# First token tiles of a layernorm, GLU and long-convolution kernel: loads in halves of 64 partitions, VectorE copies, wide warm-up matmuls, another issue order

## The chip, the cores and the metric

The kernel runs on one core of a Trainium2 chip. TensorE (PE) multiplies matrices, VectorE (DVE) and ScalarE (ACT) work on elements and empty PSUM, SyncE (SP) issues nearly all DMA transfers; ScalarE issues a few at the start. The metric is the device time of one execution in microseconds (us). Three executions of the kernel before took 243.47, 243.84 and 244.39 us; their median, 243.84 us, is the time before.

## The reference

A sequence of 2048 tokens of 640 channels goes through a layernorm. The normalised tokens `xn` feed two branches, and the result is the sum of the input and both:

```python
x  = A_q                                     # (1, 2048, 640) bf16
xn = _layernorm(x)
out = x + _A_ref(xn, A_k, A_v, ...) + _B_ref(xn, B_w_gate, B_w_up, B_w_down)

def _A_ref(q, k, v, shift_k, ssm_k, ssm_D):
    kv = causal_conv4(k, shift_k) * v        # per channel, 4 taps
    y  = irfft(rfft(kv) * rfft(ssm_k))       # causal convolution over 2048 positions
    return q * (y + kv * ssm_D)

def _B_ref(x, w_gate, w_up, w_down):         # 640 -> 1728 -> 640
    return (sigmoid(x @ w_gate) * (x @ w_up)) @ w_down
```

## The kernel before

**Tiling.** The 2048 tokens are 16 tiles of 128 (`acc[:, m, :]`, one row of 640 channels on each partition). Partition 32q+n of tile m holds token 64n+16q+m, which is why a tile's load is written as four pieces of 32 partitions, one for each q (`load_x`, line 365). Four tiles make a group `tr`; there are four groups.

**Branch B.** For a group, the four normalised tiles are transposed into `xnT` (640 channels on the partitions, 512 tokens). Group 0 is transposed on PE (`rec_tp`, five 128x128 transposes to a tile at line 704, then one copy from PSUM to `xnT0`, lines 328 and 329); groups 1 to 3 are written to DRAM and read back with a transposing DMA (line 698). Then 14 column blocks `fc` of gate and up are multiplied (`rec_fc`, line 773, five matmuls of 512 columns for each of gate and up), evacuated by a sigmoid on ACT (line 734) and a product on DVE (line 736) into `hT`, and multiplied by the down weights (`rec_down`, line 789). Blocks 0 and 1 of group 0 are done tile by tile instead (`rec_first`, line 752), so that PE can begin when the first token tile is there.

**Branch A.** The convolution is a two-step Fourier transform as matmuls, in ten slices: `rec_st1` (line 508), `rec_st2` (line 528), products on DVE, `rec_st3` (line 576), and `rec_st4` (line 608) at the end.

**Order.** Every piece of work is recorded as an operation with the buffers it reads and writes (`_Plan.op`). The list `ORDER` gives the order in which all operations are emitted; `ON_DVE` names those that may run on ACT or DVE and run on DVE. Each engine runs its own operations strictly in that order, and so does each queue of DMA issues. A PSUM tile of tag `g` (two slots) or `c` (three slots) has to be emptied before its slot is used again. DMA issues use eight semaphores in turn: an issue waits until the transfer issued eight before it has landed.

**The start, where the change is.** A memset makes a zero tile, and PE multiplies it 61 times with 84 columns (`warm`, line 818, operation `("wps", 0)`). Tiles 0 and 1 of the tokens are loaded in quarters, q = 0 and 1 from SP, q = 2 and 3 from ACT; tiles 2 and 3 come together, in quarters from SP. On SP the fourth piece of tiles 0 and 1 stands behind the first gate weights, and the pieces of tiles 2 and 3 behind that. Statistics of tiles 0 to 2 are taken by DVE (`rec_stat`: two `bn_stats` at line 638 and one `bn_aggr` at 640), those of tile 3 by ACT (`rec_stat_act`: a sum at line 645 and a sum of squares at 651). `rec_fast` is a square root on ACT (line 656) and a reciprocal on DVE (658); `rec_norm` (682) normalises on DVE. The copies of the transposes of tiles 0 and 2 are on ACT, those of 1 and 3 on DVE. A second set of 12 zero matmuls of 85 columns follows the first transpose.

Of the kernel before, what the change touches and what calls it, by code (L numbers as in the profile page):

```python
# [44 lines left out]
def _dft_tables():  # L45
# [31 lines left out]


ORDER = [
# [38 lines left out]
]  # L118
ON_DVE = [
    38, 47, 101, 105, 138, 139, 141, 145, 148, 150, 181, 183, 198, 221, 319, 412, 439, 446, 469, 483, 487, 505, 517, 808  # L120
]


# [94 lines left out]
def kernel(  # L218
# [116 lines left out]
    def dma(fn, nd, run, q="SP", few=0.0, **kw):  # L335
        few = few or (1.4 if nd <= 64 and run > 1000 else 1.0)
        plan.op({q: (0.48 + nd / 8000.0, lambda: fn(nc.sync if q == "SP" else nc.scalar))},
                size=1.05 * few * nd * (10.6 + run / 23.8) / 16e3 + 0.03, nd=nd, **kw)
# [26 lines left out]
    def load_x(q, m0, m1, eng, pri):  # L365
        dma(lambda e: e.dma_start(acc[32 * q:32 * q + 32, m0:m1, :], xq4[q][:, m0:m1, :]), 32, 1280 * (m1 - m0), q=eng,  # L366
            w=[("acc", m, q) for m in range(m0, m1)], pri=pri)

    def weight(tr, n):
        tr = 0 if tr == 1 else tr  # L370
# [272 lines left out]
    def rec_stat_act(m0, m1, pri):  # L643
        for m in range(m0, m1):
            plan.op({"ACT": (0.75, lambda m=m: nc.scalar.activation(jk, acc[:, m, :], ACT.Identity,  # L645
                                                                    accum_out=st[:, TMP, m:m + 1]))},
                    r=[("acc", m, q) for q in range(4)] + [("jk",)], w=[("sum", m)], pri=pri)
        act(100, lambda: nc.scalar.activation(st[:, MEAN, m0:m1], st[:, TMP, m0:m1], ACT.Copy, scale=1.0 / DM),
            r=[("sum", m) for m in range(m0, m1)], w=[("mean", m) for m in range(m0, m1)], pri=pri)
        for m in range(m0, m1):  # L650
            plan.op({"ACT": (0.75, lambda m=m: nc.scalar.activation(jk, acc[:, m, :], ACT.Square, scale=-1.0,
                                                                    bias=st[:, MEAN, m:m + 1], accum_out=st[:, VAR, m:m + 1]))},
                    r=[("acc", m, q) for q in range(4)] + [("mean", m), ("jk",)] + ([("sd", 1)] if m == 3 else []), w=[("mv", m)], pri=pri)

    def rec_fast(m, pri, scale=1.0):
        act(100, lambda: nc.scalar.activation(st[:, TMP, m:m + 1], st[:, VAR, m:m + 1], ACT.Sqrt, bias=eps, scale=scale),
# [80 lines left out]
                r=[pk(1), (sg,)], w=[(hk, fc)], pri=pri - 2000)  # L737

    MG, MD = 213.5, 135.0
    WARM = (61, 84)  # L740

    def rec_first(pri):
        every = [(fc, u) for fc in range(2) for u in range(2)]
# [62 lines left out]
    FIX = -1e6  # L806
# [9 lines left out]
    def warm(n, w=512):  # L816
        for _ in range(n):
            nc.tensor.matmul(tl["wps"][:, 0, 0:w], lhsT=tl["warm"][:, 0:P], rhs=tl["warm"][:, 0:w], start=True, stop=True)
    plan.op({"PE": (4.4, lambda: warm(*WARM))}, r=[("warm",)], w=[("wps", 0)], alloc=[("wps", "c")], pri=FIX)
    for m in range(2):  # L820
        for q in range(2):
            load_x(q, m, m + 1, "SP", FIX)
            load_x(q + 2, m, m + 1, "ACT", FIX)
    load_w(0, 0, FIX + 2)
    load_w(0, 1, FIX + 2)
    for q in range(4):
        load_x(q, 2, 4, "SP", FIX + 1)
    dma(lambda e: e.dma_start(FEt, Fdram.ap()[:, 2 * K1:]), 128, 256, w=[("FE",)], pri=11.0, nb=9.0)
    dma(lambda e: e.dma_start(Ft[:], Fdram.ap()[:, 0:2 * K1]), 128, 128, w=[("F",)], pri=12.0, nb=9.0)
    load_D(10.0)  # L830
# [17 lines left out]
    rec_fast(3, FIX + 50, 1.0 / DM)  # L848
    rec_norm(0, FIX + 5, True)
    rec_tp(0, FIX, True)  # L850
    plan.op({"PE": (1.5, lambda: warm(12, 85))}, r=[("warm",), ("xn0", 0)], w=[("wps", 1)], pri=FIX + 0.5)
    for m0, m1, k in ((4, 8, "LS1"), (8, NQ, "LNS")):
        if m0 == 4:
            for m in range(m0, m1):
# [77 lines left out]
```

## Time and profile before

| | us |
|---|---|
| median of three executions | 243.84 |
| the profiled execution: its own time | 244.01 |
| the profiled execution: span from first to last instruction | 242.2 |
| PE busy | 232.5 |
| DVE busy | 198.4 |
| ACT busy | 152.0 |
| first matmul of `rec_first` (line 752) starts | 7.87 |
| first matmul of `rec_fc` (line 773) starts | 14.13 |
| last matmul ends | 236.78 |

The profile is of one execution. Times in it run from its first instruction; 1.8 us of the execution's own time lie outside the span. The granted clock is the share of full speed that the throttle gave to TensorE. "DMA share" is the mean busy share of the core's 16 DMA engines in a stretch of time.

### The profile page before, as it was taken

The page shows a single profiled execution, that of the slowest core. Times are in us where ns is not written, and L with a number is a line of the kernel's source. Part 1 is how long each engine was busy: PE and PEld are TensorE (multiplying, and loading weights), DVE is VectorE, ACT ScalarE, POOL GpSimd, SP SyncE. Part 2 cuts the span into 40 slices and gives each one's busy share as a digit, 9 for nine tenths or more (in the row PEclk, how much of TensorE's full clock was granted, in tenths as well). Part 3 has the DMA queues.
Part 4 walks back from the last instruction along what each step waited for, and adds up shares of the span by engine and source line. Part 5 has one row for each costly group of instructions (what it writes and reads, how often), then busy time and mean ns, then how long its engine had stood idle before and what let it go on. Part 6 is the DMA issues. An engine that isn't in the chain of part 4 may idle for free.

```text
span 242.2 us, 8395 instructions
## 1 busy us (share of the span) xinstructions
PE 232.5 (96%) x3739; PEld 142.7 (59%) x3739; DVE 198.4 (82%) x281; ACT 152.0 (63%) x213; POOL 0.7 (0%) x6
## 2 busy tenths in 40 slices
PE   7799999999999999999999999999999999999990
PEld 7764445774445556766646455777665645456760
DVE  3616975697899998999999998898988799879971
ACT  2542333058777999167998989879797752663310
POOL 1000000000000000000000000000000000000000
PEclk9799999999999999999999999999999999999998
DMA  5999999999989699996998794399561888520771
GB/s 156 271 232 283 238 220 214 283 160 150 184 157 191 103 185 189 192 289 86 158 199 185 201 187 156 87 299 151 147 168 22 216 245 296 141 83 3 202 243 48
DMA packets 92667, 43.72 MB, mean 180 GB/s; under 512 B 69720, under 2 KB 89112, under 8 KB 92312
## 3 DMA queue, kind: packets, MB, share of 16 engines
q1 hardware_dynamic: 92440, 43.04, 80.8%
q8 instruction: 29, 0.48, 0.8%
q10 hardware_dynamic: 192, 0.16, 0.2%
q14 instruction: 6, 0.05, 0.1%
HBM read 30.74 MB, written 5.24 MB: 149 GB/s over the span
## 4 chain that ended last, share of the span: by engine, by line
PE 87%; DMA 5%; ACT 3%; DVE 1%; issue 1%; SPq 1%; ACTq 0%
PE g L773 47%; PE g L789 19%; PE c L528 9%; DMA acc<-in_A_q_dram 5%; PE c L576 4%; PE c L508 3%; PE c L752 3%; PE c L608 2%; ACT VV L645 2%; SPq L366 1%; PE g L704 0%; DVE bs L638 0%; DVE VV L682 0%; DVE hT L736 0%; ACT xnT L328 0%
## 5 line engine op out<-in xcount | busy, mean ns | idle before, releaser
L773 PE MATMUL g<-xnT,w 128*128 128x512 bf16 x380 | 88.6, 380 | 0.4 <-ACT sig L734 0.4
L789 PE MATMUL g<-wd,hT 128*128 128x320 bf16 (+2 forms) x462 | 65.0, 295 | 0.0
L773 PEld LDWEIGHTS <-w 128*128 128x128 bf16 x380 | 35.3, 98 | 40.0 <-issue 1.0
L789 PEld LDWEIGHTS <-hT 128*128 128x128 bf16 x462 | 43.0, 98 | 17.0 <-issue 0.2
L328 ACT CAST S<-c 128x1024 bf16<-128x1024 f32 (+2 forms) x41 | 39.8, 1001 | 9.5 <-PE c L528 5.3
L736 DVE TENSOR_TENSOR hT<-sig,g 128x512 bf16<-128x512 bf16 x44 | 30.1, 685 | 16.3 <-PE g L773 14.7
L734 ACT ACTIVATE sig<-g 128x512 bf16<-128x512 f32 x44 | 26.2, 601 | 25.2 <-PE g L773 23.0
L773 PE MATMUL g<-xnT,VV 128*128 128x512 bf16 x140 | 32.2, 379 | 0.0
L328 ACT CAST T<-c 128x1024 bf16<-128x1024 f32 (+1 forms) x21 | 20.6, 1009 | 9.7 <-PE c L508 6.3
L482 DVE TENSOR_TENSOR P<-kt,sT 128x2048 bf16<-128x2048 bf16 x20 | 24.3, 1221 | 0.2
L528 PEld LDWEIGHTS <-Mt 64*128 64x128 f16 x1280 | 19.8, 95 | 5.7 <-issue 5.4
L528 PE MATMUL c<-T,Mt 64*128 64x64 bf16 x1280 | 22.2, 190 | 0.5 <-issue 0.5
L773 PEld LDWEIGHTS <-VV 128*128 128x128 bf16 x140 | 13.3, 98 | 15.0
L800 DVE TENSOR_TENSOR acc<-g,acc 128x320 bf16<-128x320 f32 (+2 forms) x33 | 15.7, 479 | 7.3 <-PE g L789 7.0
L328 ACT CAST VV<-c 128x1024 bf16<-128x1024 f32 x17 | 17.0, 1019 | 4.9 <-PE c L576 4.7
L331 ACT ACTIVATE T<-c 128x1024 bf16<-128x1024 f32 x18 | 18.1, 1026 | 1.3 <-PE c L508 1.3
L645 ACT ACTIVATE VV<-acc 128x640 bf16<-128x640 bf16 x9 | 6.6, 737 | 12.2 <-DMA acc<-in_A_q_dram 12.1
L560 DVE TENSOR_TENSOR S<-S 64x2048 bf16<-64x2048 bf16 x10 | 12.2, 1220 | 0.3
L557 DVE TENSOR_TENSOR S<-S 128x2048 bf16<-128x2048 bf16 x10 | 12.2, 1224 | 0.3
L562 DVE TENSOR_TENSOR S<-P 64x2048 bf16<-64x2048 bf16 x10 | 12.2, 1222 | 0.3
L486 DVE TENSOR_TENSOR P<-P,P 128x2048 bf16<-128x2048 bf16 x10 | 12.2, 1223 | 0.2
L550 DVE TENSOR_TENSOR P<-S,P 128x2048 bf16<-128x2048 bf16 x10 | 12.2, 1220 | 0.0
(75 smaller groups left out, 183.0 us busy)
## 6 DMA issues: line engine op xcount, KB each, us to landing
P<-S SPq DMA_DIRECT2D x20, 256.0 KB, 3.8
w<-in_B_w_up_dram SPq DMA_DIRECT2D x7, 640.0 KB, 6.3
w<-in_B_w_gate_dram SPq DMA_DIRECT2D x7, 640.0 KB, 6.3
kt<-in_A_k_dram SPq DMA_DIRECT2D x8, 320.0 KB, 7.9
xnd<-VV SPq DMA_DIRECT2D x4, 640.0 KB, 5.4
vt<-in_A_v_dram SPq DMA_DIRECT2D x8, 320.0 KB, 7.2
VV<-in_A_ssm_k_dram SPq DMA_DIRECT2D x16, 96.0 KB, 4.1
wd<-in_B_w_down_dram SPq DMA_DIRECT2D x3, 480.0 KB, 8.9
```

What stands on the lines that cost most here:

```text
L328: fa = lambda: nc.scalar.copy(out=out_fn(), in_=in_fn())
L331: fa = lambda: nc.scalar.activation(out_fn(), in_fn(), ACT.Copy, scale=scale)
L482: dve(2048, 2, lambda: nc.vector.tensor_tensor(tl[c].rearrange("p i (n c) -> p i n c", c=CJ), two(t), sh(t), ALU.mult), r=kr + [("s",)], w ...
L486: dve(2048, 2, lambda: nc.vector.tensor_tensor(tl[a][:], tl[a][:], tl[b][:], ALU.add), r=[(b,)], w=[(a,)], pri=pri)
L528: nc.tensor.matmul(tl[c][:, b, 64 * kk:64 * kk + 64], lhsT=Mb[rows, k, 64 - 64 * r:192 - 64 * r], rhs=tl[T][rows, 2 * k + r].rearrange("p ...
L550: dve(n, 2, lambda: nc.vector.tensor_tensor(Q(), X(), Q(), ALU.mult), r=[(Z, "h", 0), (Z, "h", 1)], w=[(Z, 0)], pri=pri)
L557: dve(n, 2, lambda: nc.vector.tensor_tensor(X(), X(), H(), ALU.mult), r=[(Z, 0)] + sr, w=[(S_, "p")], pri=pri + 0.01)
L734: act(512, lambda: nc.scalar.activation(tl[sg][:], pv(0), ACT.Sigmoid), r=[pk(0)], w=[(sg,)], alloc=[(sg, "sig")], pri=pri - 2000)
L736: dve(512, 1, lambda: nc.vector.tensor_tensor(hT[:, fc, :], tl[sg][:], pv(1), ALU.mult), r=[pk(1), (sg,)], w=[(hk, fc)], pri=pri - 2000)
L773: nc.tensor.matmul(tl[c][:], lhsT=w()[:, k, o:o + P], rhs=tl[X][:, k, :], start=(k == 0), stop=(k == NC - 1))
L789: nc.tensor.matmul(tl[pd[i]][:, 0:d1 - d0], lhsT=hT[:, fc, t4 * P:(t4 + 1) * P], rhs=wd[:, fc, d0:d1], start=(fc == 0), stop=(fc == NFC - 1))
L800: dve(d1 - d0, 1, lambda i=i, m=m, pd=pd, d0=d0, d1=d1: nc.vector.tensor_tensor(acc[:, m, d0:d1], tl[pd[i]][:, 0:d1 - d0], acc[:, m, d0:d1 ...
```

## The change

It loads tiles 0 to 3 of the tokens with a new function, `load_x2`, in halves of 64 partitions: the first half of each from SP, the second from ACT, tile 0, tile 1, then tiles 2 and 3 together; all six issues stand ahead of the weights on their queues. The source of such a half is a pattern of three steps in DRAM: 2 blocks q, 32 rows n, and the channels. Each piece had been a pattern of 32 rows and the channels. The warm-up is 9 matmuls of 512 columns and, after the first transpose, one more of 512. A wait of tile 3's sum of squares for tile 1's square root is gone. There are six operations fewer, and `ORDER` and `ON_DVE` are new throughout.

```diff
 ORDER = [
-    5, 1, 6, 8, 7, 10, 9, 13, 11, 12, 20, 0, 73, 74, 75, 76, 17, 19, 77, 93, 78, 79, 80, 18, 81, 4, 82, 94, 98, 106,
+    1, 0, 4, 5, 6, 7, 8, 10, 67, 68, 69, 72, 73, 70, 71, 2, 74, 87, 9, 82, 75, 92, 77, 83, 11, 13, 16, 12, 58, 14, 76,
...
 ]
 ON_DVE = [
-    38, 47, 101, 105, 138, 139, 141, 145, 148, 150, 181, 183, 198, 221, 319, 412, 439, 446, 469, 483, 487, 505, 517, 808
+    41, 93, 97, 99, 135, 138, 140, 144, 145, 223, 250, 271, 327, 438, 440, 441, 447, 457, 461, 477, 802
 ]
...
+    def load_x2(h, m0, m1, eng):
+        dma(lambda e: e.dma_start(acc[64 * h:64 * h + 64, m0:m1, :], xq4[2 * h:2 * h + 2][:, :, m0:m1, :]), 64,
+            1280 * (m1 - m0), q=eng, few=1.0, w=[("acc", m, q) for m in range(m0, m1) for q in (2 * h, 2 * h + 1)], pri=FIX)
...
-                    r=[("acc", m, q) for q in range(4)] + [("mean", m), ("jk",)] + ([("sd", 1)] if m == 3 else []), w=[("mv", m)], pri=pri)
+                    r=[("acc", m, q) for q in range(4)] + [("mean", m), ("jk",)], w=[("mv", m)], pri=pri)
...
-    WARM = (61, 84)
...
-    plan.op({"PE": (4.4, lambda: warm(*WARM))}, r=[("warm",)], w=[("wps", 0)], alloc=[("wps", "c")], pri=FIX)
-    for m in range(2):
-        for q in range(2):
-            load_x(q, m, m + 1, "SP", FIX)
-            load_x(q + 2, m, m + 1, "ACT", FIX)
+    plan.op({"PE": (9 * 0.43, lambda: warm(9))}, r=[("warm",)], w=[("wps", 0)], alloc=[("wps", "c")], pri=FIX)
+    for m0, m1 in ((0, 1), (1, 2), (2, 4)):
+        for h in range(2):
+            load_x2(h, m0, m1, "ACT" if h else "SP")
     load_w(0, 0, FIX + 2)
     load_w(0, 1, FIX + 2)
-    for q in range(4):
-        load_x(q, 2, 4, "SP", FIX + 1)
...
-    plan.op({"PE": (1.5, lambda: warm(12, 85))}, r=[("warm",), ("xn0", 0)], w=[("wps", 1)], pri=FIX + 0.5)
+    plan.op({"PE": (0.43, lambda: warm(1))}, r=[("warm",), ("xn0", 0)], w=[("wps", 1)], pri=FIX + 0.5)
```

The new order at the start, as each engine and queue of the built program has it:

| | order |
|---|---|
| SP queue | half 0 of tile 0, of tile 1, of tiles 2 and 3; first halves of the gate and up weights; table `F`; second half of the gate weights; a quarter of tiles 4 to 7; second half of the up weights; table `FE`; then the other quarters of tiles 4 to 7, and the weights of blocks 4 to 7 |
| ACT | half 1 of tile 0, of tile 1, of tiles 2 and 3; square root of tile 0; sum of tile 3; square root of tile 1; mean, sum of squares and square root of tile 3; copy of the transposes of tile 1; square root of tile 2; sigmoids |
| DVE | statistics of tile 0; `bn_stats` of tile 1; reciprocal of tile 0; a memset; `bn_aggr` of tile 1; normalise tile 0; first `bn_stats` of tile 2; reciprocal of tile 1; normalise tile 1; copy of the transposes of tile 0; second `bn_stats` of tile 2; reciprocal of tile 3; `bn_aggr` of tile 2; normalise tile 3; reciprocal of tile 2; normalise tile 2; copies of tiles 2 and 3 |
| PE | 9 zero matmuls; transposes of tile 0; 1 zero matmul; transposes of tile 1; `rec_first` of tile 0 (gate, up) and tile 1 (up); transposes of tiles 2 and 3; the rest of `rec_first` but two groups; `rec_fc` of blocks 2, 3, 6, 4, ... |

Later, three operations net move from DVE to ACT (253 on DVE and 196 on ACT, from 256 and 193), and the order of matmul groups differs in many places.

74 rows, old and new, of the table ORDER are left out of this document.

## The prediction

> **What bounds the kernel now.** I read the page first (busy shares, then the chain that ended last), then the chain in order of time, the timeline of DVE at the start, and stages of the span.
>
> ```profile
> PE 232.5 (96%) x3739; PEld 142.7 (59%) x3739; DVE 198.4 (82%) x281; ACT 152.0 (63%) x213; POOL 0.7 (0%) x6
> PE 87%; DMA 5%; ACT 3%; DVE 1%; issue 1%; SPq 1%; ACTq 0%
> ```
>
> TensorE is the path. The chain in order of time shows where it is not:
>
> ```profile
> 0.73 2.06 DMA acc<-in_A_q_dram
> 2.81 2.95 DMA acc<-in_A_q_dram
> ...
> 14.30 9.71 PE g L773 x45
> 24.84 15.12 PE g L773 x70
> 43.87 7.25 DMA acc<-in_A_q_dram
> 57.81 4.48 PE g L773 x20
> ```
>
> From 14.13 us (first `rec_fc` matmul) to 236.78 PE runs with hardly a gap: 45 matmuls in 9.71 us is 216 ns each. The sum of all groups after 14.13 at their undisturbed times in this trace (104 x 1.08 us for `rec_fc`, 62 x 0.95 and a few short ones for `rec_down`, 20 x 0.345 at L508, 40 x 0.477 at L528, 20 x 0.447 at L576, 5.1 at L608, and 5.5 for going from one kind to another, some 0.1 each) is 219.6 us of the 222.6 there are. So a new order of that stretch can win 3 us at the most; everything else must come from the first 14 us, which go from token load to statistics to transposes to `rec_first`:
>
> ```profile
> 3.42 0.89 DVE L638 BATCH_NORM_STATS2 bs<-acc 128x6 f32<-128x320 bf16 x2 [2.26 <-DMA acc<-in_A_q_dram]
> 5.78 0.89 DVE L638 BATCH_NORM_STATS2 bs<-acc 128x6 f32<-128x320 bf16 x2 [0.22 <-DMA acc<-in_A_q_dram]
> ```
>
> Tile 0 is there at 3.4, tile 1 at 5.76, since its fourth quarter stands behind a weight load on SP. Both waits end with a DMA.
>
> ```profile
> 8.00:11.40 3.40, 3.40 (x35) 3.40 (x34) 2.49 (x9) 2.15 (x7) 0.00 (x0) 0.50 0.97 301
> 4.40:5.00 0.60, 0.60 (x18) 0.60 (x16) 0.24 (x2) 0.29 (x1) 0.00 (x0) 1.00 1.13 366
> 228.00:230.00 2.00, 2.00 (x17) 1.46 (x15) 1.97 (x3) 0.00 (x0) 0.00 (x0) 1.00 1.13 396
> 238.20:239.10 0.90, 0.00 (x0) 0.00 (x0) 0.00 (x0) 0.00 (x0) 0.00 (x0) 1.00 0.27 78
> 239.20:239.90 0.70, 0.00 (x0) 0.00 (x0) 0.00 (x0) 0.00 (x0) 0.00 (x0) 1.00 0.29 84
> ```
>
> These are stages; the last three numbers are granted clock, DMA share and GB/s. First row: PE at half clock while it does `rec_first`. The clock changes in this trace at 4.59, 8.01, 11.42 and 240.11 only: a grid of 3.41 us. The last two rows matter most.
>
> **The load in halves.** In those two rows only the final stores of tile 15 are running. Each has 128 rows and, on its DRAM side, a pattern whose outermost step counts 4 (q), and it gets 0.27 to 0.29 of the 16 engines: four of them. The transfers of the other rows have 32 or 128 outermost and fill all 16. The DMA view agrees:
>
> ```profile
> acc<-in_A_q_dram ACTq DMA_DIRECT2D x4, 40.0 KB, 2.6
> out_dram<-acc SPq DMA_DIRECT2D x4, 40.0 KB, 1.6
> out_dram<-acc SPq DMA_DIRECT2D x1, 80.0 KB
> ```
>
> The last has no landing time, because marks are missing: of the eight semaphores that tell of landings, five end 11 marks short of 16 to a transfer, and each of these five has exactly one transfer with 4 outermost on it (the three final stores, the loads of `A_shift_k` and `A_ssm_D`); the other three are complete. The new halves have 2 outermost (two blocks q, then 32 rows). I read this as two engines for each. The three final stores, issued at 236.85, 237.59 and 238.25, run one behind the other at one share, so few-engine transfers use the same engines; I take it that both queues' halves share one pair.
>
> The Trainium skill says so too ("DMA: Bandwidth & Descriptors", section "Why a DMA increments its semaphore by 16 and not by 1"): a transfer runs on the largest number of engines up to 16 that divides the outermost counts of both sides, on this path the lowest-numbered ones. For 2 and 64 that is two, the same two for SP and ACT, and the trace's 4-outermost transfers agree with it. With its figure of 27 GiB/s an engine the tiles would, as an estimate, land some 3 us sooner than below.
>
> Rate of one engine: 366/16 = 22.9 GB/s (the load row), 396/16 = 24.8 as the upper end, 78/4 = 19.5 as the lower. I take the load row, as it is of token loads. Tiles 0 to 3 are 512 rows of 1280 bytes, 0.655 MB: at 45.8 GB/s 14.3 us (13.2 to 16.8). The first packet moves at 1.8 (1.77 in the trace), and a landing is told some 0.6 after its last. So tile 0 lands at 1.8 + 3.6 + 0.6 = 6.0 instead of 3.4, tile 1 at 9.6 instead of 5.8, tiles 2 and 3 at **16.7** (15.6 to 19.2) instead of about 7.
>
> **Who waits.** DVE has `bn_stats` of tile 1 ahead of the reciprocal and normalisation of tile 0, and the first `bn_stats` of tile 2 ahead of tile 1's normalisation and tile 0's copy; ACT has tile 3's sum ahead of tile 1's square root. So no `rec_first` matmul starts before tiles 2 and 3 are there: sum 0.93 and root 0.29 on ACT, then on DVE reciprocal 0.16, normalisation 0.45, copy 0.49 with small gaps, 2.4 us: start at **19.1** instead of 7.87. The weights are issued early, but their share on the two slow engines queues behind SP's halves: 0.33 MB/16 at 22.9 GB/s is 0.9 us each, so the gate's first half is whole at 17.6 and the up's at 18.5: hidden behind the 2.4 us.
>
> **`rec_first`.** Up to the first `rec_fc` stand 9600 columns, two sets of transposes among them (tile 1's set has been done). 20 matmuls of 128 columns take 2.08 us at half clock and 5 take 0.28 at full, so 9600 take 7.8 or 4.2 us. PE was idle, so it starts at half clock; the grid allows full clock at 21.66 (its window would be busy for 87%) or at 25.07: the end is at 24.5 or 26.1. I take **25.0**, against 14.13: **+10.9 us**.
>
> **The rest.** The warm-up has 4608 columns instead of 5124 and is over before anything waits; it costs nothing, as tile 0 lands later than its end. Copies on DVE (0.49 against 0.68 on ACT) win 0.2 each, inside the wait. Three operations net move to ACT (63% busy), no bound. The order adds one entry into L528 groups: +0.1. Later loads: eight transfers are in flight at most, and six are token halves, so the second half of the gate weights is issued near 6 and weights of blocks 4 to 7 near 19.5 (when that half is whole); with 6.9 us to land, the time of that load before, they come at 26.4 and are needed 4.6 us into `rec_fc`, at 29.6: 3 us of cover. By 25 us the queues have moved about 4.2 MB, by 14.13 before 3.1 MB: loads are ahead of PE more than before. So the stall at 57.8, where PE idles 0.4 us behind a sum of late token tiles (the 7.25 us DMA of the chain), should go: -0.4.
>
> Sum on the profiled execution's 244.01 (span 242.2 and 1.8 around it): 244.01 + 10.9 + 0.1 - 0.4 = 254.6; it was 0.17 over the median, so **254.4**. From the ends of the rate, 253 to 258; with 1.5 us for the new order either way, 251.5 to 259.5.
>
> **Rivals.** (1) *The halves spread over 16 engines, as the quarters do.* For it: 64 partitions on the SBUF side. Against: `A_shift_k` fills 128 partitions and its semaphore is still short of marks. Then tile 0 lands at 2.85 and tile 1 at 3.3; DVE goes bn_stats, aggr, bn_stats 0.92 + 0.23 + 0.92 from 2.9, then 0.16 + 0.12 + 0.21 + 0.4 to tile 0's normalisation, 0.45 + 0.16 + 0.4 and the copy 0.49: `rec_first` at 7.4 instead of 7.87, and 0.53 of tile 1's transposes lies ahead of it: 243.0. This is the other side: a gain that decides once all halves land before about 7 us. If besides the wide matmuls keep the clock up, half of 3.41 us goes too: 241.3. I doubt that: before, half clock came at 8.01 after a window in which PE was idle for 1.34 us (6.53 to 7.87) and little else; now it would be busy for about half of it. The Trainium skill ("TensorE: Matmul & The Clock Gate", section "Why this matters for your kernels") allows gaps up to about 3 us before the clock falls, which would give the 241.3; this trace's 1.34 us gap disagrees.
> (2) *SP's and ACT's halves on different pairs.* 7.2 us instead of 14.3: tiles 2 and 3 at 9.6, `rec_first` at 12.0, full clock at 14.84, `rec_fc` at 17.5: +3.4 - 0.4, 247.0. For it: nothing in the trace; against: the stores one behind the other.
> (3) *Weights late as well.* If the two slow engines hold back the loads by more than the 3 us of cover, each us more is a us: 258 and over.
>
> **Chances.** Forecast 0.72, (1) 0.14, (2) 0.08, (3) 0.06. The range reaches down to (2) and up into (3): 246.8 to 259.5. A measurement tells about 0.5% (1.2 us) from no change: of (1), 0.06 is faster by more and 0.07 within; slower 0.87.
>
> **What would show it.** Right: DMA share near 0.12 until the weights join at 3 us, first `bn_stats` near 6, second near 9.6, a third that waits till 16 or 17, first L752 matmul near 19, first L773 near 25, and from there a stretch as long as before. Wrong: first `bn_stats` before 3.5 (rival 1) or a third one before 11 (rival 2); L773 idle for weights (rival 3).

## The result, and the profile after

The changed kernel takes 255.51 us (median of 6 runs, 255.29 to 256.15), the kernel before beside it 244.12 us (6 runs). The ratio is 1.0476, with a 95% interval of 1.0424 to 1.0528: slower by 4.8%. The forecast was 254.4 us. Ratios leave out runs more than 1.5% above the fastest of their kernel, while medians keep them, and two of the profiles below, of the longer warm-up's first run and of the old warm-up, are of such runs. The profiled execution took 255.36 us, its span is 253.4 us.

The page of the changed kernel: busy shares, the shares of the chain that ended last by engine, and, from the 40 slices (6.3 us each), granted clock, DMA share and GB/s:

```profile
PE 232.4 (92%) x3676; PEld 139.4 (55%) x3676; DVE 195.4 (77%) x278; ACT 154.6 (61%) x216; POOL 0.7 (0%) x6
...
PEclk9657999999999999999999999999999999999998
DMA  2259999989996789999797678474780197820692
GB/s 71 95 141 289 264 277 292 146 231 199 157 183 100 169 146 155 203 266 292 114 231 143 156 204 200 136 196 102 191 245 6 33 231 179 298 80 7 156 238 75
...
PE 88%; DMA 6%; issue 1%; DVE 1%; ACT 1%; SPq 1%; DVEq 0%; ACTq 0%
```

PE is busy for the same 232 us as before (232.5); the span has grown by 11.2 us, and all of that is idle PE. The slices say where: in the first two the DMA engines are busy for two tenths and move 71 and 95 GB/s, and the clock is below full in the second to the fourth. (Its first recorded change, to full, is at 5.41 us, and the page counts the time before as full; the wide zero matmuls, 427 ns from one start to the next against 216 later on, show that it was half.) The chain in order of time (start, us, what) says which transfer it is:

```profile
2.19 15.01 DMA acc<-in_A_q_dram
19.76 3.03 PE c L755 x30
25.29 2.16 PE g L776 x10
27.73 14.03 PE g L776 x65
```

A token load carries the chain for 15 us, where before it was two loads of 2.06 and 2.95 us. The timeline of DVE shows the arrival of each tile as the end of a wait (start, duration, operation; in brackets the idle time before and what ended it):

```profile
7.19 0.89 DVE L642 BATCH_NORM_STATS2 bs<-acc 128x6 f32<-128x320 bf16 x2 [6.03 <-DMA acc<-in_A_q_dram]
10.80 0.89 DVE L642 BATCH_NORM_STATS2 bs<-acc 128x6 f32<-128x320 bf16 x2 [2.49 <-DMA acc<-in_A_q_dram]
17.32 0.49 DVE L642 BATCH_NORM_STATS2 bs<-acc 128x6 f32<-128x320 bf16 x1 [5.08 <-DMA acc<-in_A_q_dram]
18.90 0.48 DVE L329 COPY xnT<-g 128x640 bf16<-128x640 bf16 x1
```

Tile 0 is there at 7.2 us (3.4 before), tile 1 at 10.8 (5.8), tiles 2 and 3 at 17.3. PE waits with them (line 708 are the transposes, 755 `rec_first`, 776 `rec_fc`):

```profile
19.04 0.71 PE L708 MATMUL g<-VV 128*128 128x128 bf16 x5 [5.60 <-DVE VV L686]
19.55 3.24 PE L755 MATMUL c<-xnT,VV 128*128 128x128 bf16 x30
...
25.13 2.32 PE L776 MATMUL g<-xnT,VV 128*128 128x512 bf16 x10
```

The first `rec_fc` matmul starts at 25.13 instead of 14.13: +11.0 us. From it to the end of the last matmul (247.80) are 222.7 us, as before (222.6). The end behind that is 0.13 longer and what lies outside the span 0.2: together the 11.35 us between the two profiled executions. The loss is made before 25 us, and nothing of it is won or lost later.

Two stages in which next to nothing but the halves is on the DMA engines show how many of these they use (columns: stretch, its length, busy time of PE, PEld, DVE, ACT, POOL, then granted clock, DMA share, GB/s):

```profile
6.20:8.80 2.60, 0.00 (x0) 0.00 (x0) 1.10 (x3) 0.29 (x1) 0.00 (x0) 1.00 0.13 50
12.00:14.00 2.00, 1.14 (x6) 0.56 (x6) 0.25 (x1) 0.00 (x0) 0.00 (x0) 0.50 0.13 52
```

A share of 0.13 of 16 engines is 2.1 engines. The packets of the halves, one token row of 1280 bytes each, go at 37 to 39 a microsecond from 5 to 9 us, 49 GB/s. For two engines that is 24 each, near the 22.9 that the forecast took for one.

The DMA view cannot tell the halves from other transfers here, since in the changed kernel it has a landing time for none. The marks behind it can: a mark is a count that a transfer adds to its semaphore, and the trace keeps the time of each. The first half from SP leaves three marks. One comes at 2.06 us, before its first packet moves at 4.32, and two come at 6.53 and 7.09, behind its last packets. All six halves leave two marks behind their data, a quarter in the kernel before sixteen. The marks also show what the halves do to loads that use all engines. Of the sixteen marks of the first gate weights fourteen come from 5.7 to 6.3 us and the last two at 17.42 and 17.77; of those of the first up weights fourteen from 10.5 to 10.9 and two at 18.76 and 19.03.

### The profile page after: what moved, and what is told of

Same layout as the page of the kernel before. It is cut to its first block, busy times and chain, and to the rows that moved or that the text cites. A ratio compares the mean times of both kernels' runs of the same rounds, so it can differ in the third digit from the quotient of the medians.

```text
span 253.4 us, 8250 instructions
## 1 busy us (share of the span) xinstructions
PE 232.4 (92%) x3676; PEld 139.4 (55%) x3676; DVE 195.4 (77%) x278; ACT 154.6 (61%) x216; POOL 0.7 (0%) x6
## 4 chain that ended last, share of the span: by engine, by line
PE 88%; DMA 6%; issue 1%; DVE 1%; ACT 1%; SPq 1%; DVEq 0%; ACTq 0%
PE g L776 45%; PE g L792 24%; PE c L532 8%; DMA acc<-in_A_q_dram 6%; PE c L580 4%; PE c L512 3%; PE c L755 2%; PE c L612 2%; SPq L370 1%; PE g L708 1%; ACT VV L649 0%; DVE acc L803 0%; DVE hT L729 0%; ACT sig L727 0%; DVE VV L686 0%
## 5 line engine op out<-in xcount | busy, mean ns | idle before, releaser
L328 ACT CAST S<-c 128x1024 bf16<-128x1024 f32 (+2 forms) x39 | 37.1, 1009 | 8.5 <-PE c L532 5.8
L328 ACT CAST T<-c 128x1024 bf16<-128x1024 f32 (+1 forms) x22 | 21.3, 1008 | 7.0 <-PE c L612 3.5
L331 ACT ACTIVATE T<-c 128x1024 bf16<-128x1024 f32 x19 | 19.4, 1032 | 6.2 <-PE c L512 6.0
L328 ACT CAST VV<-c 128x1024 bf16<-128x1024 f32 x18 | 17.8, 1018 | 3.9 <-PE c L580 3.9
L642 DVE BATCH_NORM_STATS2 bs<-acc 128x6 f32<-128x320 bf16 x14 | 6.3, 479 | 13.6 <-DMA acc<-in_A_q_dram 13.6
L708 PE MATMUL g<-VV 128*128 128x128 bf16 x20 | 2.1, 264 | 12.7 <-DVE VV L686 12.7
L564 DVE TENSOR_TENSOR S<-S 64x2048 bf16<-64x2048 bf16 x10 | 12.2, 1221 | 0.3
L566 DVE TENSOR_TENSOR S<-P 64x2048 bf16<-64x2048 bf16 x10 | 12.2, 1222 | 0.3
L561 DVE TENSOR_TENSOR S<-S 128x2048 bf16<-128x2048 bf16 x10 | 12.2, 1222 | 0.2
```

What stands on the lines that cost most here:

```text
L328: fa = lambda: nc.scalar.copy(out=out_fn(), in_=in_fn())
L331: fa = lambda: nc.scalar.activation(out_fn(), in_fn(), ACT.Copy, scale=scale)
L561: dve(n, 2, lambda: nc.vector.tensor_tensor(X(), X(), H(), ALU.mult), r=[(Z, 0)] + sr, w=[(S_, "p")], pri=pri + 0.01)
L564: dve(n, 2, lambda: nc.vector.tensor_tensor(X()[lo], X()[lo], X()[hi], ALU.subtract), r=[(S_, "p")], w=[(S_, "z")], pri=pri + 0.02)
L566: dve(n, 2, lambda: nc.vector.tensor_tensor(X()[hi], Q()[lo], Q()[hi], ALU.add), r=[(S_, "z"), (Z, 0)], w=[(S_, "q")], pri=pri + 0.02)
```

## The experiments

Ten runs follow, of eight kernels (two of them ran twice). The first five undo or redo parts of the start; the last five ask whether the repaired loads lead to a faster kernel. The kernel before took 244.5 us (13 runs) beside the first four, 244.2 (17) beside the next three, 243.9 (23) beside the last three.

**Quarters in the changed kernel.** Order, copies and warm-up stay as changed; each half is issued as two transfers of 32 partitions, whose outermost step counts 32.

```diff
-        dma(lambda e: e.dma_start(acc[64 * h:64 * h + 64, m0:m1, :], xq4[2 * h:2 * h + 2][:, :, m0:m1, :]), 64,
+        def f(e):
+            for q in (2 * h, 2 * h + 1):
+                e.dma_start(acc[32 * q:32 * q + 32, m0:m1, :], xq4[q][:, m0:m1, :])
+        dma(f, 64,
...
```

> The changed kernel with one thing undone: each half of 64 partitions is issued as its two quarters of 32 partitions, at the same place of the same queue. Few engines (a pattern with 2 outermost runs on 2 of 16 DMA engines): tile 0 is there near 3 us, tiles 2 and 3 before 7, the first L755 matmul at about 7.4, the first L776 matmul at about 13.2, 243.0 us in all (241.3 if the clock also stays full). Rival, the new order's waits on DVE and ACT or another part of the change cost the time: it stays at 250 us or more.

Measured: 244.22 us (10 runs), ratio to the kernel before 0.9985 (0.9946 to 1.0023). The same bytes for the same partitions, on the same two queues:

```profile
3.85 0.89 DVE L644 BATCH_NORM_STATS2 bs<-acc 128x6 f32<-128x320 bf16 x2 [2.69 <-DMA acc<-in_A_q_dram]
5.02 0.89 DVE L644 BATCH_NORM_STATS2 bs<-acc 128x6 f32<-128x320 bf16 x2
6.37 0.49 DVE L644 BATCH_NORM_STATS2 bs<-acc 128x6 f32<-128x320 bf16 x1
```

Only the first wait is left, and the third `bn_stats` is at 6.4 instead of 17.3. So the whole loss is the pattern of the loads, and all the rest of the change together is worth nothing that this measurement can tell.

**Whole tiles.** One transfer of 128 partitions for each of tile 0, tile 1 and tiles 2 and 3, from SP alone; its outermost step counts 4.

```diff
+        def f(e):
+            if h == 0:
+                e.dma_start(acc[:, m0:m1, :], xq4[:, :, m0:m1, :])
```

> The changed kernel with each token tile loaded by one transfer of 128 partitions from SP, whose source has 4 outermost instead of 2; the ACT issues are gone. Few engines: four engines, some 100 GB/s, 6.6 us of data instead of 13; tiles 2 and 3 land at about 10, L755 starts at about 12.2, L776 at about 17.5, 247 to 248 us. Rival, two queues or half the partitions are what slows the loads, not the outermost count: tiles 2 and 3 land before 7 and the time is about 243. Rival, the waits in the new order cost it: 255.

Measured: 250.41 us (2 runs), ratio 1.0249 (1.0145 to 1.0353).

```profile
5.29 0.89 DVE L644 BATCH_NORM_STATS2 bs<-acc 128x6 f32<-128x320 bf16 x2 [4.13 <-DMA acc<-in_A_q_dram]
8.20 0.89 DVE L644 BATCH_NORM_STATS2 bs<-acc 128x6 f32<-128x320 bf16 x2 [1.77 <-DMA acc<-in_A_q_dram]
11.91 0.49 DVE L644 BATCH_NORM_STATS2 bs<-acc 128x6 f32<-128x320 bf16 x1 [2.27 <-DMA acc<-in_A_q_dram]
```

The 1280-byte packets go at 71 to 73 a microsecond between 4 and 6 us, against 37 to 39 in the changed kernel; those of 2560 bytes (tiles 2 and 3) at 38 to 40 against 20 to 21. That is four engines against two, at 23 to 27 GB/s for each, and the marks say the same: four behind the data of each whole tile, at 4.75 to 5.27 us for tile 0. The time itself was above what was expected: the first packet moves at 2.24 us and not at 1.8, the token packets take until 10.98 beside weights on the same engines (8.7 us for what twice the pair's rate would do in 7.2), and the wait ends 0.9 us behind the last one, not 0.6; so tile 2 is there at 11.9 and not at 9.6, the time that rival (2) has for twice the rate.

**One queue in halves.** ScalarE's halves as quarters, SP's as they are.

```diff
+        def f(e):
+            if h == 1:
+                for q in (2 * h, 2 * h + 1):
+                    e.dma_start(acc[32 * q:32 * q + 32, m0:m1, :], xq4[q][:, m0:m1, :])
+            else:
+                e.dma_start(acc[64 * h:64 * h + 64, m0:m1, :], xq4[2 * h:2 * h + 2][:, :, m0:m1, :])
```

> The changed kernel with ACT's halves issued as quarters, SP's halves left as they are: half the bytes remain in patterns with 2 outermost. Both queues' halves on one pair of engines: the pair now has 0.33 MB, 6.7 us, tiles 2 and 3 land near 10, L776 near 17.5, about 247 to 248 us. Each queue's halves on a pair of its own: SP's pair has as much to do as before, tiles 2 and 3 land near 17, about 255 us.

Measured: 249.73 us (2 runs), ratio 1.0221 (1.0122 to 1.0321). If each queue had a pair of its own, SP's halves would have been as late as in the changed kernel.

```profile
12.15 0.49 DVE L647 BATCH_NORM_STATS2 bs<-acc 128x6 f32<-128x320 bf16 x1 [2.88 <-DMA acc<-in_A_q_dram]
```

Tile 2 is there at 12.2 instead of 17.3, though nothing was changed on SP's queue. From 7 to 11 us its 2560-byte packets go at 14 to 17 a microsecond; in the changed kernel they had 10, and ScalarE's another 10 beside them. So the two queues' halves run on the same two engines. The changed kernel's packets say so too: both queues issue their first half at 0.73 us, but SP's first packet moves at 4.32, when ScalarE's 64 packets (from 2.16 on) are all but done. The time was above the 247 to 248 us expected, and tile 2 later than the expected 10 us: SP's packets take from 2.38 to 11.42, 9.0 us instead of 6.7. The quarters and the weights have shares on the same two engines; that this is the whole reason was not tested.

**Halves in the kernel before.** Order, copies and warm-up of the kernel before; pieces q = 0, 1 and 2, 3 of tiles 0 to 3 joined to halves.

```diff
+            h = q // 2
+            if m0 >= 4:
+                e.dma_start(acc[32 * q:32 * q + 32, m0:m1, :], xq4[q][:, m0:m1, :])
+            elif q in (0, 2 if m0 < 2 else 3):
+                e.dma_start(acc[64 * h:64 * h + 64, m0:m1, :], xq4[2 * h:2 * h + 2][:, :, m0:m1, :])
```

> The kernel before, its order and its warm-up, with tiles 0 to 3 loaded in halves of 64 partitions (the first issue of a pair carries the half, the second is left out; all of tiles 2 and 3 on SP as before). Few engines: tile 0 near 7 us, tile 1 near 11, tiles 2 and 3 near 17; the up weights wait behind these on SP, L752 starts near 12 but stalls, L773 starts at 22 to 25, 251 to 255 us. Rival, the new order makes the loss: 244 us, as before.

Measured: 254.76 us (2 runs), ratio 1.0427 (1.0325 to 1.0529). This one edit alone makes the loss of the whole change. It even starts `rec_first` early (12.85), and then stands:

```profile
20.02 2.32 PE L758 MATMUL c<-xnT,VV 128*128 128x128 bf16 x20 [5.42 <-DMA VV<-in_B_w_up_dram]
...
25.46 2.75 PE L779 MATMUL g<-xnT,VV 128*128 128x512 bf16 x12
```

The up weights are spread over all 16 engines, but two of their shares stand behind the halves on the slow pair: of their sixteen marks fourteen come from 11.3 to 11.8 us, the last two at 19.05 and 19.98, and PE goes on at 20.02. A transfer is there when its last share is.

**Another order, with the halves.** `ORDER` rearranged by hand: normalise, copy and first gate of tile 0, then the chain of tile 1, ahead of the statistics of tiles 2 and 3.

```diff
-    1, 0, 4, 5, 6, 7, 8, 10, 67, 68, 69, 72, 73, 70, 71, 2, 74, 87, 9, 82, 75, 92, 77, 83, 11, 13, 16, 12, 58, 14, 76,
...
+    1, 0, 4, 5, 6, 7, 8, 10, 9, 11, 13, 16, 12, 58, 14, 67, 68, 69, 70, 71, 87, 92, 100, 93, 147, 2, 72, 73, 74, 75,
...
```

> The changed kernel with its halves, but its written-out order rearranged at the start: the normalise, the copy and the first gate of tile 0, and then the chain of tile 1, stand ahead of the statistics of tiles 2 and 3 on VectorE and ScalarE. My theory: the weights that the first gate needs have their shares on the two slow engines behind the halves of SyncE's queue, and the stretch after the first content matmul needs all four tiles, so the waits that the order makes cost little: first gate not before about 17, first content matmul about 24 to 25, 253.5 to 255.5 us. Rival: the waits for the statistics of tiles 2 and 3 are what delays the path: first gate at 9 to 13, first content matmul below 20, 250 us or less.

Measured: 258.51 us (2 runs), ratio 1.0594 (1.051 to 1.0677). Two lines of PE, then one of ScalarE:

```profile
18.42 1.25 PE L747 MATMUL c<-xnT,VV 128*128 128x128 bf16 x10 [7.58 <-DMA VV<-in_B_w_gate_dram]
...
27.05 1.24 PE L768 MATMUL g<-xnT,VV 128*128 128x512 bf16 x5
```

```profile
20.24 0.69 ACT L320 COPY xnT<-g 128x640 bf16<-128x640 bf16 x1 [7.37 <-PE g L700]
```

The theory held in its main point: with tile 0 ready at 11 us the gate still waits for its weights until 18.4, only 1.1 us earlier than in the changed kernel. Fourteen of the weights' marks had come by 6.7 us, the last two came at 18.26 and 18.38. The theory missed what the new order would do instead. ScalarE now has the copy of tile 1 ahead of tile 3's sum; the copy waits for transposes, and these stand on PE behind the gate that waits for weights. So tile 3's statistics, whose data was there at 17.9, began at 20.8, and `rec_fc` came 1.9 us later than in the changed kernel.

**A longer warm-up, and the old one, with quarters.** With the loads repaired, is there a version that beats both kernels? Two edits on the version with quarters:

```diff
-    plan.op({"PE": (9 * 0.43, lambda: warm(9))}, ...
+    plan.op({"PE": (9 * 0.43, lambda: warm(13))}, ...
...
-    plan.op({"PE": (0.43, lambda: warm(1))}, ...
+    plan.op({"PE": (0.43, lambda: warm(3))}, ...
```

> The loads as quarters of 32 partitions and a longer warm-up: 13 wide matmuls ahead of the first transposes and 3 more between, so that TensorE has no pause before the first gate. If the clock stays full from its first rise on, the 3.4 us at half clock around 8.5 to 11.9 are won back by half: about 1.7 us less than the quarters alone, 242 to 242.8 us against 244.2. Rival: the clock falls all the same, or the added matmuls hold up the transposes by what they win: 244 to 245 us.

The other puts back the narrow zero matmuls:

```diff
-    ... warm(9) ... warm(1)
+    ... warm(61, 84) ... warm(12, 85)
```

> The loads as quarters of 32 partitions and the warm-up of the kernel before (61 and 12 narrow matmuls in place of 10 wide ones). Theory: the form of the warm-up costs nothing either way, 243.5 to 245 us, as the quarters with the wide matmuls. Rival: the narrow matmuls keep the sequencer of TensorE behind, and the first transposes come later by up to 1 us: 245 to 246 us.

Measured: the longer warm-up took 246.43 to 247.50 in five of six runs and 242.61 in one; no interval can be given, and its profile is of a run of 246.87. The old warm-up took 247.33 (12 runs), ratio 1.0092 (1.005 to 1.0134), its profile of a run of 248.11. Both theories fell, though the clock did what was hoped at the start. The rival of the second fell as well, as the first transposes came at 6.20 us and not later than with the wide matmuls (6.51). Here is the longer warm-up's clock by slices, and PE's waits (us in total, times, longest):

```profile
PEclk9999999999999999997999999999999999999998
```

```profile
PE g L778 <- issue: 1.8, 1, 1.8
PE g L778 <- DVE acc L805: 1.2, 1, 1.2
...
PE g L778 <- ACT sig L740: 0.7, 1, 0.7
```

The clock stayed full from 3.92 to 113.14, and `rec_fc` started at 12.19, 2 us earlier than in the first run with the quarters (14.21). But the stretch from there to the last matmul is 226.3 us instead of 222.4: pauses (those over 0.15 us) of 3.74 us instead of 1.32, and 3.41 us at half clock from 113.14 on, just behind the pause of 1.78 us, which is 1.7 us lost. With the old warm-up the same: start at 12.75, stretch 229.4, pauses of 6.2 us, and 3.41 us at half clock from 234.54 on, behind a pause of 2.15 us.

**Do the pauses belong to the program, or to the early start?** "Issue" pauses are those for which the profile shows no cause. This version makes each of the 16 wide warm-up matmuls as two of 256 columns:

```diff
-    ... warm(13) ... warm(3)
+    ... warm(26, 256) ... warm(6, 256)
```

> The quarters with the longer warm-up again, but each of its 16 wide matmuls made as two of 256 columns: the same time on TensorE, 16 instructions more in its stream. In the traces so far the pauses of TensorE that nothing in the profile explains stand at the same distance behind the first content matmul in all kernels with 10 warm-up matmuls (100, 164 and 182 us) and at other, again common, distances in those with 73 (161 and 218 us), each 2 to 3.5 us behind the start of an instruction block. Theory: they belong to the places where the instruction stream is cut into blocks, so here they move by some us against the version with 16 matmuls (44, 101, 167 us); the first content matmul stays at 12 to 13 us and the time lies between 242.5 and 248, by the pauses alone. Rival: they come from the early start itself, with the weights too late: the pauses stay at 44, 101 and 167 us and the time at 246 to 247.5.

Beside it ran the longer warm-up and the plain quarters once more:

> The quarters with the longer warm-up of 16 wide matmuls, a second time on the chip of these runs. If its 246.4 to 247.5 in five of six runs belong to the kernel, they come again: 246 to 247.5, slower than the quarters alone; if they belonged to the chip, 242 to 243, and then it beats both kernels.

> The quarters alone, a second time and beside the two versions with the longer warm-up: 243.5 to 245 us, no difference from the kernel before, with the first content matmul at 14 us where the clock falls and 12.5 where it does not.

Measured: split warm-up 247.46 (6 runs), ratio 1.0102 (1.005 to 1.0155); longer warm-up 244.67 (12 runs), ratio 1.0016 (0.998 to 1.0052); quarters alone 243.42 (12 runs), ratio 0.9984 (0.9957 to 1.0012). The pauses of the split version (those over 0.2 us) end 43.5, 99.4, 152.2, 165.8 and 216.6 us behind the first `rec_fc`: three within 1.5 us of those of the longer warm-up (44.0, 100.9, 166.8), two new ones. That is nearer to the rival, but the new ones speak against it, the time lies in both ranges (242.5 to 248, and 246 to 247.5), and the longer warm-up's second run at 244.67 fits neither of its two expectations. Of the causes, some are waits for data (the second run of the longer warm-up has 2.18 us for `P<-S`, a DMA), some are "issue". Why an earlier start brings more of both stays open. What the traces have: in four profiled executions with a longer or a narrower warm-up, `rec_fc` started at 12.0 to 12.8 us and the stretch behind it took 225.7 to 229.4 us. The quarters alone, in an execution whose clock rose at 9.51 us and then stayed full, started at 12.89 and took 222.6 (242.85 us in all): there the earlier start was kept. None of these versions beats the kernel before by more than the measurement can tell.

## Why the prediction was right

**The halves run on two engines, one pair for both queues.** Right, and shown from both sides: undone, the loss is gone; alone, it is all there; with 4 outermost the token packets go twice as fast; with one queue's halves gone, the other's come 5 us sooner; and each half leaves two marks behind its data. The reading came from a row far off in the profile, the final stores at 0.27 to 0.29 of the engines. The Trainium skill ("DMA: Bandwidth & Descriptors", section "Why a DMA increments its semaphore by 16 and not by 1") has the rule that was weighed there, and these runs agree with it for 2, 4 and 32 outermost.

**When the tiles land.** Forecast 6.0, 9.6 and 16.7, measured 7.2, 10.8 and 17.3. Three terms were mis-sized, and their errors partly cancel. By the packets in the trace, tile 0 is whole at 6.36, tile 1 at 9.92 and tiles 2 and 3 at 16.47. The rate held for the first two: 3.56 us a tile, forecast 3.58. So the data runs as if it had begun at 2.8, not at 1.8: the first half took 1.12 us to issue on ScalarE and 0.75 on SP, where the first quarter takes 0.42 and 0.41, its first packet moves at 2.16, and only 9 packets move before 3.0. That is +1.0. (So the DMA share up to 3 us was 0.07, not the 0.12 forecast.) Tiles 2 and 3 took 6.55 us instead of 7.16, -0.6: their rows are 2560 bytes, and 0.328 MB in 6.55 us is 25 GB/s an engine, near the upper end of the range (24.8) instead of the 22.9 taken. And the wait ends 0.8 us behind the last packet, not 0.6: +0.2.

**From there to `rec_fc`.** Forecast 2.4 us from the last tiles to `rec_first`, measured 2.26 (17.29 to 19.55). The claim that the order on DVE and ACT puts tiles 2 and 3 ahead of tile 0's copy is what the DVE timeline shows: the copy at 18.90, behind the third `bn_stats`. But it costs less than it seems, as the rearranged order shows: the gate's weights would have held PE until 18.4 anyhow. In the changed kernel the gate's first half was whole at 17.77 and the up's at 19.03, forecast 17.6 and 18.5: both still hidden. `rec_first` up to `rec_fc` took 5.58 us against 5.9 forecast; the clock rose at 22.48, between the two times taken (21.66 and 25.07). Its grid has the same 3.41 us step but another phase in each run. That `rec_fc` came within 0.13 us of the forecast (25.13 and 25.0) is in part luck: the tiles were 0.6 us late, and these two stretches 0.1 and 0.3 us shorter.

**The queues behind.** "The second half of the gate weights is issued near 6" was wrong: SP stood 4.81 us in the issue of the up weights at 3.49 and 5.42 us in that of table `F` at 8.35, and that half was issued at 13.81. The weights of blocks 4 to 7 went out at 20.23 (forecast 19.5) and nothing waited for them. So rival (3) did not come about.

**The stall at 57.8.** It went, as forecast; its 0.4 us did not come back in the time. The profile after has two other pauses:

```profile
PE g L776 <- issue: 1.0, 1, 1.0
PE c L532 <- issue: 0.5, 1, 0.5
```

They stand at 189 and 207 us. All pauses of over 0.15 us behind the first `rec_fc` sum to 1.44 us, before to 1.26. This term was wrong: it counted one pause, and the sum of all pauses did not fall. It is the largest part of the 0.8 us by which the profiled execution (255.36) lies above the forecast for it (254.6).

**Rival (1).** The quarters are this rival made real. It gave 243.0, or 241.3 if the clock stays up; measured were 244.22 and 243.42, against 244.5 and 243.9 for the kernel before. Its `rec_first` came at 8.41 and 7.98 instead of 7.4, as tile 0 was there at 3.85 and 3.37 rather than 2.85. The doubt on the clock was right for the first profiled execution: it fell at 8.47, behind a step of its grid (5.05 to 8.47) with 2.14 us of idle PE. In the second it had not even risen by then: the trace has its first change, to full, at 9.51. The five transposes of tile 0 show it, here of the first execution, then of the second:

```profile
6.51 0.45 PE L710 MATMUL g<-VV 128*128 128x128 bf16 x5 [1.30 <-DVE VV L688]
6.35 0.71 PE L710 MATMUL g<-VV 128*128 128x128 bf16 x5 [1.11 <-DVE VV L688]
```

The same work takes 0.45 us at full and 0.71 us at half clock. The second execution lost only the stretch up to 9.51, the first that from 8.47 to 11.88, so its `rec_fc` started at 12.89 instead of 14.21.

## What to carry to other kernels

Before joining small transfers into larger ones, read the outermost count of each side of the pattern: 32 rows outermost filled the engines here, 2 blocks outermost put the same bytes on two engines, though on two queues, and 4 blocks on four, though on 128 partitions. A transfer that is slow on two engines also holds up wide transfers queued behind it, as each of those waits for its last share. And when PE is the bound of the rest, test whether a start made earlier is kept at the end: here 2 us were not, while 1.3 us in one execution of the quarters were.

## What the runs showed of the hardware that was not expected

A transfer on two engines was slow to issue as well: 0.75 and 1.12 us for the first ones and 0.50 to 0.69 for the other four, against 0.32 to 0.45 for a quarter of the kernel before. Issues behind them took 4.8 and 5.4 us. In the kernel before no issue ahead of 20 us took more than 1.6, but one at 20.66 took 5.1, so long issues are not a mark of few engines alone.

The clock can fall in the middle of a kernel, after a pause much shorter than one step of its grid: behind pauses of 1.78 us (longer warm-up), 2.18 us (its second run) and 2.15 us (old warm-up) came 3.41 us at half clock. This is the stage behind the first of them:

```profile
113.20:116.50 3.30, 3.30 (x9) 1.15 (x8) 1.62 (x2) 1.50 (x2) 0.00 (x0) 0.50 0.67 160
```

PE is busy throughout, at half clock. Behind 1.88 us (old warm-up, until 57.9) and 1.72 us (split warm-up, until 177.8) it did not fall. What differs is where the pause lies on the grid. With steps of 3.41 us laid out from the changes in each trace, the first three pauses lie whole in one step, and the other two straddle two steps, with 1.01 and 0.88 us of idle PE in them, and 0.55 and 1.22. The twelve traces together give a rule with one exception: behind a step at full clock with up to 1.63 us of idle PE the clock stayed full, and behind one with 1.73 us or more, about half a step, it fell. The exception is a step of the rearranged order (22.62 to 26.03) with 1.92 us, behind which it stayed full. In the kernel before, the step ahead of the fall at 8.01 had 1.73 us, a pause of 0.39 and one of 1.34. The rise takes a busier step: at half clock, steps with up to 0.78 us of idle PE were followed by full clock, those with 0.86 us or more by half.

The Trainium skill ("TensorE: Matmul & The Clock Gate", section "Why this matters for your kernels") advises against gaps of more than about 3 us; in these runs less than 2 was enough.
